# A dense layer as seven block products instead of eight: Strassen's scheme in the second layer of an FFT-plus-hardswish kernel

## The chip, the core and the metric

The kernel runs on one core of a Trainium2 chip. Its engines are TensorE (PE in the profile; PEld is its weight load), VectorE (DVE), ScalarE (ACT), GpSimd (POOL) and SyncE (SP), each with its own instruction queue, worked off in order; 16 DMA engines move data. The metric is the device time of one execution in microseconds (us), as the median of several runs. Everything is f32; TensorE runs each f32 matmul as two passes, so the profile counts two MATMUL and two LDWEIGHTS instructions for each matmul of the code.

## The reference

```python
# x: (8, 3008, 256) f32; w_in: (256, 2048); w_out: (2048, 256), both f64
X = np.fft.fft(np.fft.fft(x, axis=1), axis=2).real.astype(np.float32)
h = X.reshape(8 * 3008, 256) @ w_in
g = h * np.clip(h + 3.0, 0.0, 6.0) / 6.0
out = (g @ w_out).astype(np.float32)          # (24064, 256)
```

Two discrete Fourier transforms, of length 3008 over the sequence and 256 over the features, of which the real part is kept, then two dense layers with a hardswish between them. The second dense layer, g @ w_out, is what the change recasts.

## The kernel before, in words

**Transforms.** The sequence transform is split as 3008 = 47 x 64. The eight batches are worked off in four pairs (class Pair). Stage 1 (load_x, fold, stage1) takes the 47-point transform as a matmul with a constant matrix F: load_x (L97) brings a piece of 8 of the 64 columns n2 on GpSimd's DMA queue, fold (L102) adds and subtracts mirrored features on VectorE for the first pair and on GpSimd for the others, stage1 (L114) multiplies, ScalarE copies out of PSUM, and SP stores the piece to a tensor zd in DRAM. Stage 2 (load_g, stage2, stage2n_mul, stage2n_sum, L131 to L167) reads zd back in groups by output frequency k1 (load_g, on GpSimd's queue), takes the 64-point transform with the data as stationary operand, and leaves q and a correction row qn in SBUF; the small product m of stage2n_mul runs on VectorE. The feature transform never runs by itself: fold_w_in multiplies it into the first layer's weights at the start (W1, and WN for the one feature that is handled apart).

**The dense layers.** A pair's tokens come in 6 chunks (class Chunk) of 8 rows k1 x batch with 64 tokens each, and each chunk stands for twice its 512 tokens: by symmetry u + v is the layer's input sum for one frequency and u - v that of the mirrored one. For each block fc of 128 of the 2048 hidden features a step does this:

- mlp1 (L177): u and v, one matmul of 512 columns each, into one PSUM bank each (ps_h, one buffer of each); VectorE forms s = u + WN * qn (L189), h[0] = s + v (L191) and h[1] = s - v, tokens reversed (L193), all to SBUF; ScalarE forms t = relu(h / 6 + 0.5) for both (L195).
- gate (L198): a = min(t, 1) * h on VectorE, twice (L202), t and h both in SBUF.
- mlp2 (L206): eight matmuls, each with 128 tokens of a as stationary operand and the 256 columns of W2 of this fc as moving operand (L213), summed over the 16 fc in four PSUM banks. After the last fc ScalarE copies each bank out (L222) and SP stores it in rows of 1 KB (L230, L233). The last chunk of a pair has six k1 rows in its mirrored half, so seven matmuls.

**The order** is written out by hand. Step number s runs over 4 pairs x 6 chunks x 16 fc = 384. In each step the program emits, in this order: what beside() has put there for this step, mlp1 of step s + 2, gate of step s + 1, mlp2 of step s. Each engine's queue follows that order. beside() spreads the other work over the steps: for the first pair the reading (load_w_out) and narrowing (narrow_w_out) of the w_out blocks 2 to 7 at steps 0 to 11; in every pair the load of the next g groups and their stage 2; and for the pair that comes next, its load_x, its folds on GpSimd and its stage 1.

**The start.** Before step 0 the kernel loads constants and the first pair's x, runs its stage 1, and loads and narrows w_in. The weights arrive as f64; narrow (L259) turns one block of 512 columns into f32 with eight VectorE operations (L271 to L278) on SBUF. Blocks 0 and 1 of w_out are narrowed before step 0, straight into W2.

Of the kernel before, what the change touches and what calls it, by code (L numbers as in the profile page):

```python
# [26 lines left out]

N1, N2 = 47, 64
NK1 = (N1 + 1) // 2


@with_exitstack
def kernel(
# [14 lines left out]
    NFC = FF // P  # L48
    NP = B // 2
    PR, PZ = 2 * N1, 4 * NK1  # L50
    XC = 8
    NXC = N2 // XC
    KC = 8
# [3 lines left out]
    assert NXC == 2 * FF // 512 and NFC % 2 == 0  # L57
    assert S == N1 * N2 and D == 2 * P and B % 2 == 0 and TB == 512 and NK1 % KK == 0
# [5 lines left out]
    wpool = ctx.enter_context(tc.tile_pool(name="wpool", bufs=1))  # L64
# [3 lines left out]
    hpool = ctx.enter_context(tc.tile_pool(name="hpool", bufs=2))  # L68
    apool = ctx.enter_context(tc.tile_pool(name="apool", bufs=3))
    opool = ctx.enter_context(tc.tile_pool(name="opool", bufs=4))  # L70
# [6 lines left out]
    out_k = out.rearrange("(b k2 k1) d -> b k2 k1 d", b=B, k1=N1)  # L77
# [3 lines left out]
    F = consts.tile([PR, PZ], F32, name="F")  # L81
# [4 lines left out]
    W2 = consts.tile([P, NFC, D], F32, name="W2")  # L86
# [26 lines left out]

    def stage1(pr, c, i):  # L114
# [6 lines left out]
        ps = ps_d.tile([P, 2, D], F32, tag="d", name="ps1")  # L121
        nc.tensor.matmul(ps[0:PZ], F[:], y[:, 2 * i:2 * i + 2, :], start=True, stop=True)  # L122
# [8 lines left out]
    def load_g(pr, ck):  # L131
        g = gpool.tile([P, 2, KK, D], F32, tag="g", name="g")
        for b in range(2):
            nc.gpsimd.dma_start(  # L134
                out=g[:, b],
                in_=pr.zd[b].rearrange("k c n d -> (c n) k d")[:, ck * KK:(ck + 1) * KK, :],
            )
        pr.g[ck] = g

    def stage2(pr, ck, i):  # L140

        if i == 0:
            pr.q[ck] = qpool.tile([P, 2, KC, N2], F32, tag="q", name="q")
        g = pr.g[ck]
        ps = ps_d.tile([P, 2, 4, N2], F32, tag="d", name="ps2")
        for u in range(4):
            kk, b = 2 * i + u // 2, u % 2
            for blk in range(2):
                nc.tensor.matmul(ps[:, blk, u], g[:, b, kk, blk * P:(blk + 1) * P],  # L149
                                 T[:, blk, ck * KK + kk], start=True, stop=True)  # L150
        nc.scalar.copy(pr.q[ck][:, :, 4 * i:4 * i + 4, :], ps[:])  # L151

    def stage2n_mul(pr, ck):

        m = spool.tile([P, KK, 2, N2], F32, tag="m", name="m")
        t0 = T[:, 0, ck * KK:(ck + 1) * KK, :].unsqueeze(2).to_broadcast([P, KK, 2, N2])
        gn = pr.g[ck][:, :, :, P:P + 1].rearrange("p b k o -> p k b o").to_broadcast([P, KK, 2, N2])
        nc.vector.tensor_tensor(m[:], t0, gn, op=AL.mult)
        pr.pr[ck] = m

    def stage2n_sum(pr, ck):
        m = pr.pr.pop(ck)
        ps = ps_d.tile([P, TB], F32, tag="d", name="ps3")
        nc.tensor.matmul(ps[:], ones[:], m[:].rearrange("p k b n -> p (k b n)"), start=True, stop=True)  # L164
        pr.qn[ck] = qpool.tile([P, TB], F32, tag="qn", name="qn")
        nc.scalar.copy(pr.qn[ck][:], ps[:])  # L166
        del pr.g[ck]  # L167

    class Chunk:
        def __init__(self, pr, ck):  # L170
            self.pr, self.ck = pr, ck
            self.nm = KC - 2 if ck == NCK - 1 else KC

            self.tiles = [(0, j) for j in range(KC // 2)] + [(1, j) for j in range(self.nm // 2)]
            self.h, self.t, self.a, self.acc = {}, {}, {}, {}

    def mlp1(ch, fc):  # L177
        q, qn = ch.pr.q[ch.ck], ch.pr.qn[ch.ck]
        fs = slice(fc * P, (fc + 1) * P)
        u = ps_h.tile([P, TB], F32, tag="u", name="u")  # L180
        v = ps_h.tile([P, TB], F32, tag="v", name="v")
        nc.tensor.matmul(u[:], W1[:, 0, fs], q[:, 0], start=True, stop=True)  # L182
        nc.tensor.matmul(v[:], W1[:, 1, fs], q[:, 1], start=True, stop=True)  # L183
        s = spool.tile([P, KC, N2], F32, tag="s", name="s")
        h = hpool.tile([P, 2, KC, N2], F32, tag="h", name="h")
        t = hpool.tile([P, 2, KC, N2], F32, tag="t", name="t")
        nm = ch.nm
        v3 = v[:].rearrange("p (k n) -> p k n", n=N2)
        nc.vector.scalar_tensor_tensor(s[:].rearrange("p k n -> p (k n)"), qn[:], WN[:, fc:fc + 1], u[:],  # L189
                                       op0=AL.mult, op1=AL.add)  # L190
        nc.vector.tensor_tensor(h[:, 0], s[:], v3, op=AL.add)  # L191

        nc.vector.tensor_tensor(h[:, 1, 0:nm, ::-1], s[:, 0:nm], v3[:, 0:nm], op=AL.subtract)  # L193
        for sg, n in ((0, KC), (1, nm)):
            nc.scalar.activation(t[:, sg, 0:n], h[:, sg, 0:n], AF.Relu, bias=half[:], scale=1.0 / 6.0)  # L195
        ch.h[fc], ch.t[fc] = h, t

    def gate(ch, fc):  # L198
        h, t = ch.h.pop(fc), ch.t.pop(fc)
        a = apool.tile([P, 2, KC, N2], F32, tag="a", name="a")  # L200
        for sg, n in ((0, KC), (1, ch.nm)):
            nc.vector.scalar_tensor_tensor(a[:, sg, 0:n], t[:, sg, 0:n], 1.0, h[:, sg, 0:n],  # L202
                                           op0=AL.min, op1=AL.mult)
        ch.a[fc] = a

    def mlp2(ch, fc):  # L206
        a = ch.a.pop(fc)
        last = fc == NFC - 1
        for i, (sg, j) in enumerate(ch.tiles):

            if fc == 0 and i % 2 == 0:
                ch.acc[i // 2] = ps_a.tile([P, 2, D], F32, tag="acc", name="acc")
            nc.tensor.matmul(ch.acc[i // 2][:, i % 2],  # L213
                             a[:, sg, 2 * j:2 * j + 2, :].rearrange("p k n -> p (k n)"), W2[:, fc, :],
                             start=(fc == 0 and i % 2 == 0), stop=last, skip_group_check=True)
            if last and (i % 2 == 1 or i == len(ch.tiles) - 1):
                store(ch, i // 2)

    def store(ch, m):
        ts = ch.tiles[2 * m:2 * m + 2]  # L220
        o = opool.tile([P, 2, D], F32, tag="o", name="o")
        nc.scalar.copy(o[:, 0:len(ts)], ch.acc[m][:, 0:len(ts)])  # L222
        ks = [(ch.ck * KK + j + 1) % NK1 for _, j in ts]
        ks = [N1 - k if sg else k for (sg, _), k in zip(ts, ks)]
        for b in range(2):
            rows = out_k[2 * ch.pr.p + b]
            src = o[b * N2:(b + 1) * N2]
            if len(ks) == 2 and abs(ks[1] - ks[0]) == 1:
# [236 lines left out]
```

## Time and profile before

| | |
|---|---|
| median of 3 runs | 2261.85 us (2255.24 to 2263.06) |
| profiled execution | 2265.05 us, its span 2263.3 us |
| granted TensorE clock, mean | 0.991 |
| busy: PE, PEld | 2217.8 us, 1591.3 us |
| busy: DVE, ACT, POOL | 1389.2 us, 675.2 us, 181.4 us |
| HBM read, written | 60.07 MB, 49.81 MB |

How to read it: the chain of waits is followed back from the last instruction, at each step to what released it or to the instruction before it on its engine, so its shares tell what the time is made of. A group row gives line, engine, operation, output <- inputs, shapes and count, then the busy time and the mean length of one, then the idle time of the engine just before these instructions and what ended most of it. A timeline row gives start and length in us, the engine, line and operation, and how many instructions are merged into it. Matmuls overlap in TensorE's pipe, so the distance from one start to the next tells what they cost. An idle engine that is not on the chain costs nothing.

### The profile page before, as it was taken

The numbers are of one execution on the slowest core, as the hardware profiler recorded it, in microseconds if no ns is written. First come the engines' busy times: TensorE is split into PE (matmuls) and PEld (weight loads), VectorE is DVE, ScalarE is ACT, GpSimd is POOL, SyncE is SP. The second block draws the span as 40 slices with busy tenths as digits, with TensorE's granted clock in tenths as the row PEclk, the third lists the DMA queues.
The fourth block names the chain that finished last, engine by engine and source line by source line (L and its number), as shares of the span: only waits on it lengthen the run. The fifth ranks groups of instructions, "written<-read, shape, count | busy, mean of one in ns | idle before, by whom it ended". The sixth has DMA issues, their size and how long they took to land.

```text
span 2263.3 us, 22686 instructions
## 1 busy us (share of the span) xinstructions
PE 2217.8 (98%) x8720; PEld 1591.3 (70%) x8720; DVE 1389.2 (61%) x2097; ACT 675.2 (30%) x1077; POOL 181.4 (8%) x157
## 2 busy tenths in 40 slices
PE   6799999999999999999999999999999999999998
PEld 2467777777777777777777777777777777777776
DVE  6686656656665666655755665665566565665664
ACT  2223333232222332323222323233232232232322
POOL 0201112102000111110200111120000000000000
PEclk9799999999999999999999999999999999999999
DMA  8611112112110221111310111121101000100000
GB/s 251 194 55 47 47 50 72 51 33 79 38 30 1 61 71 54 46 33 47 84 33 17 46 47 47 47 79 33 52 19 29 26 19 25 32 19 1 19 19 17
DMA packets 39659, 111.35 MB, mean 49 GB/s; under 512 B 5440, under 2 KB 18496, under 8 KB 33344
## 3 DMA queue, kind: packets, MB, share of 16 engines
q1 hardware_dynamic: 28912, 58.51, 9.6%
q0 software_dynamic: 10496, 49.81, 7.7%
q8 instruction: 70, 1.15, 0.2%
q10 hardware_dynamic: 144, 1.57, 0.2%
q14 instruction: 37, 0.30, 0.0%
HBM read 60.07 MB, written 49.81 MB: 49 GB/s over the span
## 4 chain that ended last, share of the span: by engine, by line
PE 97%; DVE 2%; DMA 1%; issue 0%; ACT 0%; SPq 0%; POOL 0%; ACTq 0%; DVEq 0%
PE acc L213 57%; PE u L182 15%; PE v L183 15%; PE ps L122 5%; PE ps L149 4%; PE ps L164 1%; DMA st<-in_moe_w_in_dram 1%; PE wps L314 1%; DMA g<-zd 0%; DMA st<-in_moe_w_out_dram 0%; PE wns L320 0%; DVE low L272 0%; DVE ex L277 0%; DVE ex L276 0%; DVE top L271 0%; DVE frac L273 0%
## 5 line engine op out<-in xcount | busy, mean ns | idle before, releaser
L213 PEld LDWEIGHTS acc<-W,a 128*128 128x128 f32 x6016 | 1143.9, 190 | 319.7 <-issue 181.2
L213 PE MATMUL acc<-W,a 128*128 128x256 f32 x6016 | 1362.1, 379 | 0.0
L195 ACT ACTIVATE t<-h,half 128x512 f32<-128x512 f32 (+1 forms) x768 | 505.6, 705 | 1138.4 <-DVE h L191 1138.4
L189 DVE SCALAR_TENSOR_TENSOR s<-qn,WN,u 128x512 f32<-128x512 f32 x384 | 286.9, 747 | 778.4 <-PE u L182 778.4
L202 DVE SCALAR_TENSOR_TENSOR a<-t,h 128x512 f32<-128x512 f32 (+1 forms) x768 | 543.2, 749 | 0.0
L182 PE MATMUL u<-q,W 128*128 128x512 f32 x768 | 397.2, 598 | 10.4 <-DVE s L189 10.4
L183 PE MATMUL v<-q,W 128*128 128x512 f32 x768 | 394.0, 595 | 0.4 <-DVE h L193 0.4
L191 DVE TENSOR_TENSOR h<-s,v 128x512 f32<-128x512 f32 x384 | 264.2, 688 | 43.4 <-PE v L183 1.3
L183 PEld LDWEIGHTS v<-q,W 128*128 128x128 f32 x768 | 145.8, 190 | 186.4 <-issue 105.0
L193 DVE TENSOR_TENSOR h<-s,v 128x512 f32<-128x512 f32 (+1 forms) x384 | 252.7, 658 | 0.0
L182 PEld LDWEIGHTS u<-q,W 128*128 128x128 f32 x768 | 142.8, 191 | 84.6 <-issue 60.7
L122 PE MATMUL ps<-y,F 94*96 94x512 f32 x256 | 136.3, 632 | 19.7 <-DMA F<-in_c_stage_dram 15.6
L123 ACT COPY z<-ps 96x512 f32<-96x512 f32 x128 | 74.5, 582 | 225.5 <-PE ps L122 225.5
L108 POOL TENSOR_TENSOR y<-xt 94x1016 f32<-94x1016 f32 x24 | 56.3, 2345 | 973.7 <-PE ps L122 927.0
L149 PEld LDWEIGHTS ps<-T,g 128*128 128x128 f32 x768 | 96.4, 198 | 10.1 <-issue 7.3
L149 PE MATMUL ps<-T,g 128*128 128x64 f32 x768 | 94.5, 278 | 7.5 <-issue 7.2
L134 POOL DMA_DIRECT2D g<-zd x48 | 36.8, 771 | 757.5 <-PE ps L149 452.0
L122 PEld LDWEIGHTS ps<-y,F 94*96 94x96 f32 x256 | 42.4, 172 | 49.5 <-issue 25.2
L151 ACT COPY q<-ps 128x512 f32<-128x512 f32 x48 | 28.1, 586 | 149.6 <-PE ps L149 149.6
L110 POOL TENSOR_TENSOR y<-xt 94x1016 f32<-94x1016 f32 x24 | 57.4, 2393 | 0.1
L222 ACT COPY o<-acc 128x512 f32<-128x512 f32 x96 | 48.4, 575 | 5.5 <-PE acc L213 5.5
L166 ACT COPY qn<-ps 128x512 f32<-128x512 f32 x24 | 14.1, 586 | 45.2 <-PE ps L164 45.2
(30 smaller groups left out, 229.2 us busy)
## 6 DMA issues: line engine op xcount, KB each, us to landing
zd<-z SPq DMA_DIRECT2D x32, 768.0 KB, 4.3
g<-zd POOLq DMA_DIRECT2D x48, 512.0 KB, 5.1
xt<-in_x_dram POOLq DMA_DIRECT2D x32, 752.0 KB, 5.6
out_dram<-o SPq DMA_DIRECT2D x176, 128.0 KB, 2.4
st<-in_moe_w_in_dram SPq DMA_DIRECT2D x8, 512.0 KB, 8.3
st<-in_moe_w_out_dram SPq DMA_DIRECT2D x8, 512.0 KB, 5.1
T<-in_c_stage_dram ACTq DMA_DIRECT2D x1, 1536.0 KB, 9.0
out_dram<-o SPq DMA_DIRECT2D x24, 64.0 KB, 2.0
```

Source lines behind the costliest of these rows:

```text
L110: eng.tensor_tensor(y[:, :, P + 1:D], lo, hi, op=AL.subtract)
L122: nc.tensor.matmul(ps[0:PZ], F[:], y[:, 2 * i:2 * i + 2, :], start=True, stop=True)
L123: nc.scalar.copy(z[:, 2 * i:2 * i + 2, :], ps[0:PZ])
L149: nc.tensor.matmul(ps[:, blk, u], g[:, b, kk, blk * P:(blk + 1) * P], T[:, blk, ck * KK + kk], start=True, stop=True)
L182: nc.tensor.matmul(u[:], W1[:, 0, fs], q[:, 0], start=True, stop=True)
L183: nc.tensor.matmul(v[:], W1[:, 1, fs], q[:, 1], start=True, stop=True)
L189: nc.vector.scalar_tensor_tensor(s[:].rearrange("p k n -> p (k n)"), qn[:], WN[:, fc:fc + 1], u[:], op0=AL.mult, op1=AL.add)
L191: nc.vector.tensor_tensor(h[:, 0], s[:], v3, op=AL.add)
L193: nc.vector.tensor_tensor(h[:, 1, 0:nm, ::-1], s[:, 0:nm], v3[:, 0:nm], op=AL.subtract)
L195: nc.scalar.activation(t[:, sg, 0:n], h[:, sg, 0:n], AF.Relu, bias=half[:], scale=1.0 / 6.0)
L202: nc.vector.scalar_tensor_tensor(a[:, sg, 0:n], t[:, sg, 0:n], 1.0, h[:, sg, 0:n], op0=AL.min, op1=AL.mult)
L213: nc.tensor.matmul(ch.acc[i // 2][:, i % 2], a[:, sg, 2 * j:2 * j + 2, :].rearrange("p k n -> p (k n)"), W2[:, fc, :], start=(fc == 0 and ...
```

## The change

The second layer's product G @ W is split into 2 x 2 blocks and formed by the Winograd form of Strassen's scheme: seven block products in place of eight, with four sums on the side of g, four on the side of the weights and seven on the products.

- **Blocks.** A step now has two blocks of hidden features, fc and fc + 8, and a chunk 4 rows instead of 8 (KC = 4, 256 columns, 12 chunks a pair, 8 steps each: again 384 steps). The two halves of tokens are the plain and the mirrored one; the two halves of output features are interleaved in blocks of 32.
- **mlp1** runs four matmuls of 256 columns (two blocks for u, two for v). u and v are tiles of one tag with three PSUM buffers. s is formed by two VectorE operations of 256; the sum and the difference are written back over u and v in PSUM; the relus read them there; and the two gates follow at once, inside mlp1, with t in SBUF and u or v in PSUM. The mirrored half carries a minus sign, which the sums take up.
- **combine** is new: GpSimd forms the four sums of the g blocks in three operations of 512, 256 and 256 elements. It takes the place of gate in the emission order (for step s + 1, after mlp1 of step s + 2).
- **mlp2** runs seven matmuls with weights stationary (the tile G, seven combinations of w_out blocks) and 256 columns of a or c moving, 192 in a pair's last chunk. The products lie in the four banks of ps_a; after a chunk ScalarE copies them to a tile e.
- **finish** and **store** are new in this form: in the next chunk's steps 0, 1 and 2, GpSimd forms the output blocks with seven sums in five operations (finish), VectorE transposes 32 x 32 blocks (two operations for each token half), and SP stores in pieces of 256 bytes, 16 DMAs a chunk.
- **mix_w_out** is new: four VectorE and four ScalarE operations for each pair of w_out blocks form G. Narrowing now takes one block in each of steps 0 to 5, with a mix in steps 1, 3 and 5; mix 0 stands before step 0.
- **Moved or cut otherwise:** x pieces and stage 1 in units of 4 columns with three x buffers (XC = 4); load_g on SP's queue; stage2n_mul on GpSimd; one PSUM bank (ps_d) for stages 1 and 2, but the four of ps_a until step 0.

The diff, cut to its core:

```diff
-    XC = 8
+    XC = 4
-    KC = 8
+    KC = 4
...
-    xpool = ctx.enter_context(tc.tile_pool(name="xpool", bufs=2))
+    xpool = ctx.enter_context(tc.tile_pool(name="xpool", bufs=3))
...
-    ps_d = ctx.enter_context(tc.tile_pool(name="ps_d", bufs=2, space=PSUM))
-    ps_h = ctx.enter_context(tc.tile_pool(name="ps_h", bufs=1, space=PSUM))
+    ps_d = ctx.enter_context(tc.tile_pool(name="ps_d", bufs=1, space=PSUM))
+    ps_h = ctx.enter_context(tc.tile_pool(name="ps_h", bufs=3, space=PSUM))
...
-            nc.gpsimd.dma_start(
+            nc.sync.dma_start(
                 out=g[:, b],
...
-        nc.vector.tensor_tensor(m[:], t0, gn, op=AL.mult)
+        nc.gpsimd.tensor_tensor(m[:], t0, gn, op=AL.mult)
...
     def mlp1(ch, fc):
+        u = ps_h.tile([P, 2, KC, N2], F32, tag="uv", name="u")
+        v = ps_h.tile([P, 2, KC, N2], F32, tag="uv", name="v")
+        for blk, ps in ((0, u), (1, v)):
+            for i in range(2):
+                f = fc + i * NF
+                nc.tensor.matmul(ps[:, i], W1[:, blk, f * P:(f + 1) * P], q[:, blk, of:of + KC],
+                                 start=True, stop=True)
...
+        nc.vector.tensor_tensor(u[:, :, 0:ns], s[:, :, 0:ns], v[:, :, 0:ns], op=AL.add)
+        relu(t[:, 0, :, 0:ns], u[:, :, 0:ns], 1.0 / 6.0)
...
+        nc.vector.tensor_tensor(v[:, :, 0:nm], v[:, :, 0:nm], s[:, :, 0:nm], op=AL.subtract)
+        relu(t[:, 1, :, 0:nm], v[:, :, 0:nm], -1.0 / 6.0)
+        gate(a[:, 0, :, 0:ns], t[:, 0, :, 0:ns], u[:, :, 0:ns])
...
+            gate(a[:, 1, i, 0:nm, ::-1], t[:, 1, i, 0:nm], v[:, i, 0:nm])
...
+    def combine(ch, fc):
+        a = ch.a[fc][:].rearrange("p m f k n -> p (m f) (k n)")[:, :, 0:ch.n]
+        c = cpool.tile([P, 4, TB], F32, tag="c", name="c")
+        cn = c[:, :, 0:ch.n]
+        add(cn[:, 0:2], a[:, 2:3].to_broadcast([P, 2, ch.n]), a[:, 3::-3])
+        add(cn[:, 2], cn[:, 0], a[:, 0])
+        add(cn[:, 3], a[:, 1], cn[:, 2])
+        ch.c[fc] = cn
+
+    def add(out, in0, in1):
+        nc.gpsimd.tensor_tensor(out, in0, in1, op=AL.add)
...
     def mlp2(ch, fc):
+        moving = [a[:, 0], a[:, 1], a[:, 3], c[:, 0], c[:, 1], c[:, 2], c[:, 3]]
+        for i, mv in enumerate(moving):
...
+            nc.tensor.matmul(ch.acc[i // 2][:, i % 2, 0:ch.n], G[:, i, fc, :], mv,
+                             start=(fc == 0 and i % 2 == 0), stop=(fc == NF - 1), skip_group_check=True)
...
+                nc.scalar.copy(ch.e[:, k:i + 1, 0:ch.n], ch.acc[i // 2][:, 0:i + 1 - k, 0:ch.n])
+
+    def finish(ch):
...
+        add(rn[:, 0, 0], e[:, 0], e[:, 1])
+        add(wn[:, 0], e[:, 0], e[:, 5])
+        add(wn[:, 1:3], wn[:, 0:1].to_broadcast([P, 2, n]), e[:, 4:2:-1])
+        add(rn[:, 0, 1], wn[:, 2], e[:, 6])
+        add(rn[:, 1], wn[:, 1:2].to_broadcast([P, 2, n]), e[:, 2:4])
...
     def store(ch, m):
+        for h in range(2):
+            nc.vector.transpose(o[:, 0:n // DH, h], ch.r[:, m, h, 0:n].rearrange("p (j i) -> p j i", i=DH))
...
+            for qd in range(DB):
+                nc.sync.dma_start(
...
+    def mix_w_out(j):
...
+        tt(w[3], b11, b12, op=AL.subtract)
+        tt(t2[:], b22, w[3], op=AL.add)
+        tt(w[2], t2[:], b21, op=AL.subtract)
+        tt(w[4], b22, b12, op=AL.subtract)
...
             for j in range(2, NWO):
-                put(0, 2 * j - 4, narrow_w_out, j)
+                put(j - 2, narrow_w_out, ORDER[j])
...
+                if j % 2:
+                    put(j - 2, mix_w_out, j // 2)
...
         if s + AHEAD < len(steps):
             mlp1(*chunk(s + AHEAD))
         if s + 1 < len(steps):
-            gate(*chunk(s + 1))
+            combine(*chunk(s + 1))
+        if prev and fc < 3:
+            finish(prev) if fc == 0 else store(prev, fc - 1)
         mlp2(*chunk(s))
```

More of the change, by code (lines that the diff above doesn't have):

```diff
@@ L219, in store @@
-    def store(ch, m):
[L220 to L228, printed above, removed]
-                st = ks[1] - ks[0]
-                nc.sync.dma_start(out=rows[:, ks[0]:ks[0] + 2 * st:st, :], in_=src)
-            else:
-                for r, k in enumerate(ks):
-                    nc.sync.dma_start(out=rows[:, k:k + 1, :], in_=src[:, r:r + 1])
+                ch.acc[i // 2] = ps_a.tile([P, 2, TB], F32, tag="acc", name="acc")
@@ L397 @@
     mlp1(*chunk(1))
-    gate(*chunk(0))
+    combine(*chunk(0))
+    prev = None
     for s, (p, ck, fc) in enumerate(steps):
@@ L401 @@
             at = beside(p)
[L402 removed]
+        for f, a in at.get(ck * NF + fc, ()):
             f(*a)
```

263 lines of the change are left out of this document (157 added, 106 removed).

## The prediction, made before the changed kernel ran

> **What bounds the kernel now.** I read the page's head and chain first, then the groups by line, then the timeline of one steady stretch engine by engine, then the start and the end.
>
> ```profile
> span 2263.3 us, 22686 instructions
> ...
> PE 2217.8 (98%) x8720; PEld 1591.3 (70%) x8720; DVE 1389.2 (61%) x2097; ACT 675.2 (30%) x1077; POOL 181.4 (8%) x157
> ...
> PE 97%; DVE 2%; DMA 1%; issue 0%; ACT 0%; SPq 0%; POOL 0%; ACTq 0%; DVEq 0%
> PE acc L213 57%; PE u L182 15%; PE v L183 15%; PE ps L122 5%; PE ps L149 4%; PE ps L164 1%; DMA st<-in_moe_w_in_dram 1%; PE wps L314 1%; DMA g<-zd 0%; DMA st<-in_moe_w_out_dram 0%; PE wns L320 0%; DVE low L272 0%; DVE ex L277 0%; DVE ex L276 0%; DVE top L271 0%; DVE frac L273 0%
> ...
> L213 PEld LDWEIGHTS acc<-W,a 128*128 128x128 f32 x6016 | 1143.9, 190 | 319.7 <-issue 181.2
> L213 PE MATMUL acc<-W,a 128*128 128x256 f32 x6016 | 1362.1, 379 | 0.0
> L195 ACT ACTIVATE t<-h,half 128x512 f32<-128x512 f32 (+1 forms) x768 | 505.6, 705 | 1138.4 <-DVE h L191 1138.4
> ```
>
> TensorE carries 97% of the chain, 57% in the second dense layer (L213). Every f32 matmul is two passes, so L213's 6016 are 3008 matmuls. What a pass costs is read from the starts in the timeline of a steady stretch, not from the 379 ns, which overlap:
>
> ```profile
> 248.59 1.90 PE L149 MATMUL ps<-T,g 128*128 128x64 f32 x16
> 250.32 1.08 PE L182 MATMUL u<-q,W 128*128 128x512 f32 x2
> ...
> 256.41 1.02 PE L182 MATMUL u<-q,W 128*128 128x512 f32 x2
> ...
> 258.12 3.62 PE L213 MATMUL acc<-W,a 128*128 128x256 f32 x16
> ...
> 261.58 1.02 PE L182 MATMUL u<-q,W 128*128 128x512 f32 x2
> ...
> 267.61 1.02 PE L182 MATMUL u<-q,W 128*128 128x512 f32 x2
> ```
>
> A plain step is 261.58 - 256.41 = 5.17 us: 1.71 for u and v, 3.46 for 16 passes, 0.216 per pass of 256 columns. The next step, 6.03 (261.58 to 267.61), has one stage-1 matmul more (0.86). Half a stage 2 takes 1.73 (248.59 to 250.32). TensorE has no gap here; a step costs the sum of its passes.
>
> **Passes on TensorE.** The change keeps 384 steps. First layer: 8 passes of 256 columns for 4 of 512, the same columns, 1.72. Its weight loads double, but L213 already hides a 190 ns load under each 216 ns pass, so this costs nothing; if it did not hide, L213 would be slower today. Second layer: 7 products by 2 passes, 14 for 16, 3.02. A step becomes 4.74. The last of a pair's chunks now moves 192 columns: 14 x 0.216 x 0.75 = 2.26, a step 3.98 (bound: 3.02 if a narrow pass costs a full one, +24 us in all; the 64-column passes at 1.73 / 16 = 0.108 say it does not). Today's last chunk of a pair has 14 passes, by the chain of waits near the end:
>
> ```profile
> 2241.95 3.02 PE acc L213 x14
> ```
>
> Before: 320 x 5.17 + 64 x 4.74 = 1958. After: 352 x 4.74 + 32 x 3.98 = 1796. **-162 us.** Stages 1 and 2 keep their passes.
>
> **VectorE's step.** The timeline of one step, VectorE's add and the relu on ScalarE that it releases:
>
> ```profile
> 2000.48 0.69 DVE L191 TENSOR_TENSOR h<-s,v 128x512 f32<-128x512 f32 x1
> ...
> 2001.26 1.33 ACT L195 ACTIVATE t<-h,half 128x512 f32<-128x512 f32 x2 [3.84 <-DVE h L191]
> ```
>
> The gates now stand in mlp1, behind their own relu. From these rows: s in two halves about 0.95 (0.86 today, L189 to L191 below, plus 0.1 for one more instruction); relu starts 0.78 after the add, takes 0.7, about 0.1 to signal, so gate 0 starts 1.6 after the add and gate 1 ends at 2.9. Together 3.85, plus four transposes of 256 a chunk (no row; half of a 0.69 op each, 0.18 a step). Queued behind the waiting gates is only the next step's s, which waits for TensorE anyway. 4.0 under 4.74: hidden. The add and subtract now write PSUM, which no row shows: between nothing more (L191 reads PSUM at the usual 0.6) and twice as long (+1.2 a step: 5.2, over the 5.0 of steps without stage 1, +44 us). I take the first.
>
> **GpSimd's step**, the new load and the dearest unknown. The timeline of GpSimd in one fold (two sums, two DMA issues between them, a small copy, the next load's issue):
>
> ```profile
> 243.66 2.34 POOL L108 TENSOR_TENSOR y<-xt 94x1016 f32<-94x1016 f32 x1 [40.84 <-PE ps L122]
> 245.95 1.56 POOL L134 DMA_DIRECT2D g<-zd  x2
> 247.53 2.36 POOL L110 TENSOR_TENSOR y<-xt 94x1016 f32<-94x1016 f32 x1
> 249.81 0.70 POOL L111 COPY y<-xt 94x16 f32<-94x16 f32 x1
> 250.46 0.57 POOL L99 DMA_DIRECT2D xt<-in_x_dram  x1
> ```
>
> 1016 elements take 2.29 start to start. Pure proportion gives 1.15 for 512 and 0.58 for 256. If the copy of 16 (0.65) is all fixed cost, 512 cost 1.46 and 256 cost 1.05. That copy jumps 128 elements at each one and the adds run straight, so I stay nearer the first: 1.28 and 0.76. A combine (512 + 256 + 256, two waits on itself at 0.1) is 3.0 (2.5 to 3.8); a finish (2 x 512, 3 x 256) 5.2 (4.1 to 6.5) a chunk. In a chunk that also folds: 8 x 3.0 + 5.2 + two folds of about 3.2 and their load issues (0.57 each) + half a mul (0.65) = 37.4. TensorE's chunk there: 8 x (4.74 + 0.43 stage 1 + 0.27 stage 2 with its sum) = 43.5. Hidden on average. Locally: at the start of every second chunk the queue holds load, combine, finish, then mul (moved here, in front of the next combine): 0.2 + 0.57 + 3.0 + 5.2 + 1.3 + 3.0 = 13.3 us after the step began (0.2 is when the first combine's gates are done). The products that need this second combine come two steps later, behind u, v and three products of a alone: 2 x 5.44 + 1.72 + 1.29 = 13.9. Without load and stage 1 it is 12.7 against 2 x 5.0 + 3.0 = 13.0. A margin of about nothing; I add **+5** (0.2 us at 24 such starts).
>
> The Trainium skill (GPSIMD Engine Reference, section 3.1) gives 4497 ns for an add of 2048 and advises VectorE for such work. With 2.29 at 1016 that makes an estimate of 2.7 to 2.8 a combine; by it the sum would stay without the +5.
>
> **Do the two engines hold each other up?** VectorE's timeline beside that same fold, and one pair of gates (253.50) with no fold beside it:
>
> ```profile
> 244.48 0.75 DVE L189 SCALAR_TENSOR_TENSOR s<-qn,WN,u 128x512 f32<-128x512 f32 x1 [2.69 <-PE u L182]
> 245.34 0.69 DVE L191 TENSOR_TENSOR h<-s,v 128x512 f32<-128x512 f32 x1
> ...
> 246.54 4.52 DVE L202 SCALAR_TENSOR_TENSOR a<-t,h 128x512 f32<-128x512 f32 x2
> ...
> 253.50 1.29 DVE L202 SCALAR_TENSOR_TENSOR a<-t,h 128x512 f32<-128x512 f32 x2
> ```
>
> While GpSimd folds, the ops with one operand in PSUM run at their usual 0.75 and 0.69, but two gates with both inputs in SBUF take 4.52 for 1.29. The new gates read u or v from PSUM and t from SBUF, L189's form, so by these rows they pass freely. The Trainium skill (SBUF — State Buffer, "SBUF: two separate sides") says that GpSimd and a VectorE op with two SBUF inputs lock each other out for a whole instruction; this trace agrees (+3.23 us for two gates). It speaks against the start, where w_out is still narrowed and mixed beside the combines.
>
> **The start.** The chain of waits, then the timeline:
>
> ```profile
> 75.98 5.49 DMA st<-in_moe_w_out_dram
> ```
> ```profile
> 89.35 0.42 DVE L271 TENSOR_SCALAR top<-st 128x512 int32<-128x512 int32 x1
> ...
> 93.46 0.42 DVE L271 TENSOR_SCALAR top<-st 128x512 int32<-128x512 int32 x1
> ...
> 96.53 1.43 PE L182 MATMUL u<-q,W 128*128 128x512 f32 x2
> ...
> 101.60 0.74 DVE L189 SCALAR_TENSOR_TENSOR s<-qn,WN,u 128x512 f32<-128x512 f32 x1
> ...
> 107.94 2.43 POOL L108 TENSOR_TENSOR y<-xt 94x1016 f32<-94x1016 f32 x1 [6.40 <-DMA xt<-in_x_dram]
> 108.09 2.56 DVE L271 TENSOR_SCALAR top<-st 128x512 int32<-128x512 int32 x1
> ...
> 117.91 0.74 DVE L189 SCALAR_TENSOR_TENSOR s<-qn,WN,u 128x512 f32<-128x512 f32 x1
> ...
> 122.28 4.79 PE L213 MATMUL acc<-W,a 128*128 128x256 f32 x16
> ```
>
> A narrow alone is 4.1 (89.35 to 93.46); beside folds 9.8 (108.09 to 117.91), its own time plus GpSimd's two folds: they add. Today six narrows lie in steps 0 to 10 and TensorE runs unbroken from 122.28, having done four u,v pairs and one second-layer step, 10.3 us: 112 us lost. After: load_g moves to SP's queue and the mul to GpSimd, so the first two narrows no longer wait for g and start when their rows land (81.5), end near 90, mix 0 (four ops, no row; 0.42 each from half a 0.69 op and a signal: 1.7) near 92, and s(0) waits only for u: 98 instead of 101.6. Two steps of VectorE: 105.6. Then a narrow stands in each of steps 0 to 5, ahead of mlp1, and a mix in every second. Each combine becomes ready just as VectorE starts narrowing, so they take turns: 6 x (4.1 + 3.85 + 3.0) + 3 x 1.7 + 5.6 (two load issues, mul, fold, by turns too) = 76 us, to 182. By then TensorE has done 8 x 1.72 + 0.86 + 6 x 3.02 + 1.7 + 1.7 = 36 us: 146 lost. **+34 us** (with no turn-taking 24 less). Stage 1 of pair 0 has the same passes and bytes in smaller pieces, with more PSUM banks; +-4.
>
> **The end and the queues.** SP's last output issues (timeline), the end of the last pass (chain), and the page's DMA parts:
>
> ```profile
> 2254.24 1.13 SPq L230 DMA_DIRECT2D out_dram<-o  x2
> ```
> ```profile
> 2255.33 0.02 issue
> ```
> ```profile
> out_dram<-o SPq DMA_DIRECT2D x176, 128.0 KB, 2.4
> ...
> q1 hardware_dynamic: 28912, 58.51, 9.6%
> ```
>
> From the last pass (2255.3) to the end are 8 us. After: copy 0.3, the first half of a 192-column finish 2.9, two transposes 0.6, 16 issues at 0.57 = 9.1, landing 2.4, signals about 1: 16 to 17. **+9 us.** Inside, 16 issues a chunk (9 us of 40) and the moved load_g leave SP's queue free. The output goes in 96,256 pieces of 256 bytes; q1's packet takes 0.096 x 2263 x 16 / 28912 = 0.12 us of an engine, at most a third of the 16 engines: hidden.
>
> **Sum**, against the profiled execution's 2265.05: -162 + 34 + 9 + 5 = 2151. The median of the runs is 3.2 lower: **2148 us.**
>
> **The rivals.**
> *GpSimd becomes the bound* (all dear ends: combine 3.8, finish 6.5, fold 3.55, mul 1.46): its folding chunk takes 45.5 against 43.5, and 24 such chunks (8 in each of three pairs) cost 48 us; in the other 24 the second combine ends at 15.6 behind a mul and 14.2 without, against 13.0, on average 1.9 late, 46 us. In place of the 5: 2148 + 89 = 2237. For: the margins above. Against: the straight adds.
> *VectorE becomes the bound* (PSUM writes twice as long): 2148 + 44 = 2192. Against: PSUM reads cost nothing extra.
> *The port is shared after all* (slower): the gates wait for GpSimd as L202 did. +3.23 a step makes VectorE 7.3; 376 steps from 182 and 17 at the end, about 2930. It decides from 1.4 us a step (a step of 5.49 would equal today's time). For: L202's row. Against: L189 and L191 beside the same fold.
> *The change saves no TensorE time*: the passes can be counted in the diff, 14 for 16; only a pass that costs more than 0.216 could undo it, and L213 has the same shape. No chance of its own.
>
> **How the numbers follow.** Forecast (TensorE stays the bound, 2119 to 2180) 0.66; GpSimd 0.18; VectorE 0.06; shared port, or a wait among the three u,v banks of that size, 0.10. The range goes from the start without turn-taking and without local stalls (2148 - 24 - 5 = 2119) to 2220, which takes in the VectorE case and the cheaper three quarters of GpSimd's; with a little of the forecast lost at either end about 0.8 lies in it. All but the last are faster by over 0.5%, which is about what a measurement of this kernel can tell from no change; a mild form of the last, or GpSimd dearer than priced, could land within it: faster 0.88, same 0.03, slower 0.09.
>
> **What would show it.** Right: second-layer passes 5376 (4928 of 256 columns, 448 of 192) at 0.216 start to start, plain steps of 4.74 in the last pair, PE over 95% of the chain after about 182 us, gates near 0.7 beside a busy GpSimd, combines near 3.0. Wrong: idle before the products released by POOL (c) or before v released by DVE, gates of over 1 us in the middle of the run, a first unbroken stretch that starts far from 182, or a tail far from 17.

## The result, and the profile after

| | before | after |
|---|---|---|
| median | 2262.45 us (4 runs, 2255.24 to 2267.87) | 2138.09 us (4 runs, 2136.32 to 2139.95) |
| profiled execution, its span | 2265.05 us, 2263.3 us | 2137.45 us, 2135.5 us |
| busy: PE, DVE, POOL | 2217.8, 1389.2, 181.4 us | 2067.8, 1489.9, 1424.5 us |

The changed kernel takes 0.9452 of the time before [0.9424, 0.948]: 124 us less, where 114 were forecast. The page's head and chain, and the passes of the second layer by shape:

```profile
PE 2067.8 (97%) x9616; PEld 1752.6 (82%) x9616; DVE 1489.9 (70%) x2785; ACT 707.4 (33%) x1221; POOL 1424.5 (67%) x1629
...
PE 90%; DVE 5%; DMA 2%; issue 1%; ACT 1%; SPq 0%; POOL 0%; DVEq 0%; POOLq 0%; ACTq 0%
```
```profile
L272 PE MATMUL acc<-c,G 128*128 128x256 f32 x2816 | 666.1, 379 | 0.0
L272 PE MATMUL acc<-a,G 128*128 128x256 f32 x2112 | 518.0, 382 | 0.0
L272 PE MATMUL acc<-c,G 128*128 128x192 f32 x256 | 46.8, 326 | 0.0
L272 PE MATMUL acc<-a,G 128*128 128x192 f32 x192 | 36.4, 326 | 0.0
```

TensorE is still the engine that sets the end. Its second-layer passes are 4928 of 256 columns (2816 + 2112) and 448 of 192. None of these four groups waited: the idle time in the last column is 0.0. GpSimd went from 8% to 67% busy, and stands at 0% in the chain.

One plain step in the timeline:

```profile
2003.71 1.03 PE L218 MATMUL u<-q,W 128*128 128x256 f32 x4
2004.02 1.27 POOL L262 TENSOR_TENSOR c<-a 128x512 f32<-128x512 f32 x1 [1.87 <-PE acc L272]
...
2004.78 0.87 DVE L223 SCALAR_TENSOR_TENSOR s<-qn,WN,u 128x256 f32<-128x256 f32 x2 [0.90 <-PE u L218]
...
2005.44 1.46 PE L272 MATMUL acc<-a,G 128*128 128x256 f32 x6
2005.75 0.70 DVE L231 TENSOR_TENSOR u<-s,v 128x512 f32<-128x512 f32 x1
2006.17 0.73 POOL L262 TENSOR_TENSOR c<-a,c 128x256 f32<-128x256 f32 x1
2006.73 1.89 PE L272 MATMUL acc<-c,G 128*128 128x256 f32 x8
...
2007.94 0.68 DVE L250 SCALAR_TENSOR_TENSOR a<-t,v 128x512 f32<-128x512 f32 x1
2008.46 1.90 PE L173 MATMUL ps<-T,g 128*128 128x64 f32 x16
```

From u at 2003.71 to the next work at 2008.46 are 4.75 us: 1.73 for u and v, 1.29 for six passes, 1.73 for eight. VectorE works from 2004.78 to 2008.62, 3.84 us, and its second gate takes 0.68. GpSimd's combine takes 2.88 (2004.02 to 2006.90). Both lie inside TensorE's step.

The stretches table, for the whole run between start and tail and for two chunks in which GpSimd also folds (a stretch begins where u of a chunk's first step begins):

```profile
core 0: us, PE busy (x) PEld busy (x) DVE busy (x) ACT busy (x) POOL busy (x), PEclk, DMA share, GB/s
170.00:2122.00 1952.00, 1949.49 (x9242) 1679.78 (x9242) 1352.77 (x2536) 662.44 (x1136) 1379.70 (x1573) 1.00 0.17 44
716.96:760.18 43.22, 43.22 (x202) 36.51 (x201) 28.99 (x52) 14.89 (x25) 33.38 (x39) 1.00 0.19 49
760.18:804.26 44.08, 44.08 (x204) 36.89 (x203) 29.00 (x52) 15.49 (x26) 32.38 (x38) 1.00 0.26 72
```

TensorE is busy for 1949.49 of 1952.00 us (and has 97% of the chain there), and for the whole of each folding chunk, in which GpSimd works 32 to 33 us.

The start and the end, in the chain of waits:

```profile
75.84 7.09 DMA g<-zd
...
92.31 0.89 DVE s L223 x2
...
99.77 0.34 DVE top L349
...
106.62 0.80 DVE s L223 x2
...
133.45 0.34 DVE top L349
...
139.57 0.34 DVE G L390
...
166.62 2.04 PE v L218 x4
```
```profile
2115.57 6.51 PE acc L272 x40
```

The first narrowing among the steps begins at 99.77 and VectorE lets TensorE run unbroken from 166.62: 67 us for six steps with their narrowing, combines and three mixes. The last pass ends at 2122.08 (2115.57 + 6.51), 13.4 us ahead of the end.

### The profile page after: what moved, and what is told of

Its sections match the earlier page's. It is cut to its first block, busy times and chain, and to the rows that moved or that the text cites. A ratio compares the mean times of both kernels' runs of the same rounds, so it can differ in the third digit from the quotient of the medians.

```text
span 2135.5 us, 29238 instructions
## 1 busy us (share of the span) xinstructions
PE 2067.8 (97%) x9616; PEld 1752.6 (82%) x9616; DVE 1489.9 (70%) x2785; ACT 707.4 (33%) x1221; POOL 1424.5 (67%) x1629
## 3 DMA queue, kind: packets, MB, share of 16 engines
q1 hardware_dynamic: 144768, 83.72, 14.4%
## 4 chain that ended last, share of the span: by engine, by line
PE 90%; DVE 5%; DMA 2%; issue 1%; ACT 1%; SPq 0%; POOL 0%; DVEq 0%; POOLq 0%; ACTq 0%
PE acc L272 51%; PE v L218 15%; PE u L218 15%; PE ps L145 4%; PE ps L173 4%; PE ps L189 1%; DVE a L250 1%; DMA st<-in_moe_w_in_dram 1%; ACT t L247 1%; DVE u L231 1%; DVE s L223 0%; DVE frac L351 0%; DVE low L350 0%; DVE ex L353 0%; DMA xt<-in_x_dram 0%
## 5 line engine op out<-in xcount | busy, mean ns | idle before, releaser
L262 POOL TENSOR_TENSOR c<-a 128x512 f32<-128x512 f32 (+1 forms) x384 | 478.6, 1246 | 559.2 <-PE acc L272 295.8
L272 PE MATMUL acc<-c,G 128*128 128x256 f32 (+1 forms) x3072 | 713.0, 375 | 0.0
L223 DVE SCALAR_TENSOR_TENSOR s<-qn,WN,u 128x256 f32<-128x256 f32 x768 | 334.3, 476 | 440.2 <-PE u L218 435.5
L272 PEld LDWEIGHTS acc<-c,G 128*128 128x128 f32 x3072 | 578.5, 190 | 73.2
L272 PE MATMUL acc<-a,G 128*128 128x256 f32 (+1 forms) x2304 | 554.4, 377 | 0.0
L272 PEld LDWEIGHTS acc<-a,G 128*128 128x128 f32 x2304 | 437.9, 192 | 57.8
L218 PE MATMUL v<-q,W 128*128 128x256 f32 x1536 | 401.0, 384 | 27.9 <-DVE a L250 27.9
L218 PE MATMUL u<-q,W 128*128 128x256 f32 x1536 | 397.6, 381 | 0.0
L262 POOL TENSOR_TENSOR c<-a,c 128x256 f32<-128x256 f32 (+1 forms) x384 | 276.5, 720 | 30.1
L262 POOL TENSOR_TENSOR c<-c,a 128x256 f32<-128x256 f32 (+1 forms) x384 | 275.4, 717 | 30.1
L231 DVE TENSOR_TENSOR u<-s,v 128x512 f32<-128x512 f32 (+1 forms) x384 | 263.0, 685 | 42.5 <-DVE s L223 2.3
```

What stands on the lines that cost most here:

```text
L218: nc.tensor.matmul(ps[:, i], W1[:, blk, f * P:(f + 1) * P], q[:, blk, of:of + KC], start=True, stop=True)
L223: nc.vector.scalar_tensor_tensor(s[:, i].rearrange("p k n -> p (k n)"), qn[:, of * N2:(of + KC) * N2], WN[:, f:f + 1], u[:, i].rearrange(" ...
L231: nc.vector.tensor_tensor(u[:, :, 0:ns], s[:, :, 0:ns], v[:, :, 0:ns], op=AL.add)
L262: nc.gpsimd.tensor_tensor(out, in0, in1, op=AL.add)
L272: nc.tensor.matmul(ch.acc[i // 2][:, i % 2, 0:ch.n], G[:, i, fc, :], mv, start=(fc == 0 and i % 2 == 0), stop=(fc == NF - 1), skip_group_c ...
```

## Experiments

The theory: TensorE's passes set the time; seven products are worth their share of them because everything added lies under TensorE's step, and what is given back lies in the start and the tail. The rivals: the shared port (gates with both inputs in SBUF) or GpSimd's load would undo the gain. The ratios below are against the kernel before, run on the same chip, with a 95% interval.

**The scheme alone undone.** Everything else of the rewrite stays (chunks of 256 columns, outputs turned over, stores of 256 bytes):

```diff
-        for i, mv in enumerate(moving):        # seven products
+        for q in range(2):
+            for f in range(2):                 # eight plain ones, for both m
+                nc.tensor.matmul(ch.acc[m][:, q, 0:ch.n], G[:, 2 * f + q, fc, :], a[:, 2 * m + f],
...
-            combine(*chunk(s + 1))
...
-    finish(prev)
```

> The changed kernel with only the scheme undone: eight plain block products a step, no combine, no finish, the rest (256-column steps, gates from PSUM, transposes, start) as changed. If the gain is the passes that TensorE no longer runs (theory): 352 steps x 0.431 + 32 x 0.324 = 162 us more, less about 16 at the start (narrowing no longer takes turns with combines), 7 (no mix on VectorE) and 4 at the end (no finish): 2138 + 162 - 27 = 2273, between 2260 and 2290; second-layer passes 6144 and a plain step of 5.17 us. If the gain came from the rest of the rewrite (rival): it stays near 2138, at most 2180.

Measured: 2264.98 us, 1.0005 [0.9996, 1.0015].

The rest of the rewrite comes to nothing in sum; the seven products are worth all of it, 127 us. By passes alone they would be worth more: this kernel has 5632 of 256 columns and 512 of 192, against 4928 and 448, and 704 x 0.216 + 64 x 0.163 = 162 us, 40.5 for each pair. What they give back is seen in the starts of u of the two profiled executions. The second pair begins 17.3 us later here (650.1 for 632.8) and not 40.5, so 23 us are given back by then, nearly all in the start, where combines and mixes stand beside the narrowing (the granted clock was lower there too, 0.81 for 0.91 between 80 and 180 us). Each of the next two pairs takes 39.2 us more, so 1.4 a pair are lost in a wait that the next experiment shows. The last pair and the tail give back 3.8, since the tail is 10.0 for 13.4 us (finish). Together that is 30 of the 162. The profiled executions differ by 132 and not by 127, because this kernel's was the longest of its ten runs.

**The rival that ends slower: gates with both inputs in SBUF.** The sum goes to a tile of its own and the difference over s:

```diff
+        u = spool.tile([P, 2, KC, N2], F32, tag="h", name="h")
...
-        nc.vector.tensor_tensor(v[:, :, 0:nm], v[:, :, 0:nm], s[:, :, 0:nm], op=AL.subtract)
+        nc.vector.tensor_tensor(s[:, :, 0:nm], v[:, :, 0:nm], s[:, :, 0:nm], op=AL.subtract)
+        v = s
```

> The sum and the difference go to SBUF instead of back into PSUM, so both gates have two SBUF inputs again, as in the kernel before; all else as changed. Port shared at the price of the prediction's slower rival (each pair of gates +3.23 us): VectorE's step 7 us, about 2900 us. Port shared, but a gate waits only for the rest of one GpSimd operation, and not when GpSimd is idle: gates of 0.9 to 1.5 us on average instead of 0.69, VectorE's step 4.2 to 5.2, 2145 to 2250. No sharing: gates 0.69, 2138.

Measured: 2130.89 us, 0.9414 [0.94, 0.9428]: 7 us faster than the changed kernel, where none of the three cases had it faster. The gates by groups (of 512 elements), of the changed kernel and then of this one:

```profile
L250 DVE SCALAR_TENSOR_TENSOR a<-t,u 128x512 f32<-128x512 f32 x352 | 241.8, 687 | 96.6 <-ACT t L247 91.9 <-POOL c L262 4.7
L250 DVE SCALAR_TENSOR_TENSOR a<-t,v 128x512 f32<-128x512 f32 x352 | 239.4, 680 | 0.0
```
```profile
L252 DVE SCALAR_TENSOR_TENSOR a<-t,h 128x512 f32<-128x512 f32 x352 | 311.3, 884 | 64.0 <-ACT t L249 50.7 <-POOL c L264 1.8 <-POOL r L264 0.5
L252 DVE SCALAR_TENSOR_TENSOR a<-t,s 128x512 f32<-128x512 f32 x352 | 352.1, 1000 | 0.0
```

The gates are held, as the rival says: 0.88 and 1.00 us on average against 0.69 and 0.68. But that is half a microsecond a step, not 3.23. This kernel's timeline shows why, first beside a fold and the small copy behind it, then in a plain step:

```profile
848.76 1.27 POOL L125 TENSOR_TENSOR y<-xt 94x508 f32<-94x508 f32 x1
849.47 1.12 DVE L252 SCALAR_TENSOR_TENSOR a<-t,h 128x512 f32<-128x512 f32 x1 [0.20 <-ACT t L249]
849.97 0.67 POOL L126 COPY y<-xt 94x8 f32<-94x8 f32 x1
...
1998.68 0.69 DVE L252 SCALAR_TENSOR_TENSOR a<-t,s 128x512 f32<-128x512 f32 x1
...
1999.52 1.27 POOL L264 TENSOR_TENSOR c<-a 128x512 f32<-128x512 f32 x1 [1.87 <-DVE a L252]
```

In a plain step a combine waits for its gates and is over when the next ones come, so the two keep out of each other's way by themselves. A gate is held where other work of GpSimd fills the time between, or where that work has made a combine late. In the last pair, which has no folds, nearly all held gates lie in four of a chunk's eight steps, beside the finish of the chunk before and the combines behind it. From 200 us on, 358 of the 677 gates of 512 elements last under 0.75 us. VectorE's step is then some 4.4 us on average (3.84 and the 0.52 more for two gates), still under 4.75, and TensorE's steps stay at 4.75. The lock works the other way too: the copy of 8 elements takes 0.67 us where it stands beside such a gate, and 0.20 in the changed kernel. The Trainium skill (SBUF — State Buffer, "SBUF: two separate sides") has GpSimd and such a VectorE operation lock each other out; the held gates agree, and here the lock stayed within the slack and cost no time.

Where the gain comes from is seen in a pair's last chunk, of the changed kernel and then of this one:

```profile
2110.34 1.10 PE L218 MATMUL v<-q,W 128*128 128x256 f32 x4 [0.45 <-DVE a L250]
...
2114.46 1.10 PE L218 MATMUL v<-q,W 128*128 128x256 f32 x4
```
```profile
2100.15 1.03 PE L218 MATMUL v<-q,W 128*128 128x256 f32 x4
...
2104.15 1.03 PE L218 MATMUL v<-q,W 128*128 128x256 f32 x4
```

With the gates reading PSUM, v waits for a bank until the last gate has read it (the 0.45 in brackets), and the step takes 4.12 us (2110.34 to 2114.46), in steps with transposes up to 4.69. With SBUF copies the bank is free after the difference, and the step takes 4.00. By the starts of u, the last chunks' steps give 5.6 of the 6.4 us between the two profiled executions.

**Is it GpSimd that makes the scheme pay?** The combine's three sums on VectorE instead:

```diff
-        add(cn[:, 0:2], a[:, 2:3].to_broadcast([P, 2, ch.n]), a[:, 3::-3])
+        tt = nc.vector.tensor_tensor
+        tt(cn[:, 0:2], a[:, 2:3].to_broadcast([P, 2, ch.n]), a[:, 3::-3], op=AL.add)
...
```

> The three sums of combine on VectorE instead of GpSimd. If VectorE has no room for them (theory): its step becomes 3.7 + 0.6 + 2 x 0.35 + waits 0.2 + transposes 0.2 = 5.4 us against 5.0 for TensorE in the 24 chunks without folds and 5.44 in those with: +77 us, less some 7 at the start, about 2205; more, up to 2300, if the sums (two SBUF inputs) also wait for folds and finish. If it does not matter which engine forms the sums (rival): 2138, plain steps 4.74.

Measured: 2347.52 us, 1.0376 [1.0361, 1.0392], slower than the kernel before. Head and chain of its page, and one step of its timeline:

```profile
PE 2135.1 (91%) x9616; PEld 1731.0 (74%) x9616; DVE 2136.8 (91%) x3937; ACT 697.9 (30%) x1221; POOL 444.9 (19%) x477
...
DVE 61%; PE 16%; ACT 9%; issue 5%; SPq 4%; DMA 3%; DVEq 1%; ACTq 0%; POOL 0%; POOLq 0%
```
```profile
2004.81 1.03 PE L218 MATMUL u<-q,W 128*128 128x256 f32 x4
...
2006.16 1.10 PE L218 MATMUL v<-q,W 128*128 128x256 f32 x4 [0.32 <-DVE a L250]
2006.54 0.68 DVE L257 TENSOR_TENSOR c<-a 128x512 f32<-128x512 f32 x1
...
2007.71 0.42 DVE L259 TENSOR_TENSOR c<-a,c 128x256 f32<-128x256 f32 x1
...
2010.12 1.03 PE L218 MATMUL u<-q,W 128*128 128x256 f32 x4
```

This plain step takes 5.31 us, of which VectorE's sums are 1.52 (0.68 and twice 0.42). VectorE has next to no gap left in it: it is 91% busy over the span and has 61% of the chain, and TensorE waits for it (the 0.32 in brackets, v for the bank that the gates free; 165.7 us over the run). So VectorE sets the step. I had expected about 2205, and up to 2300 if the sums also wait for folds and finish. They do wait: after 200 us the sum of 512 takes 0.68 us on average where GpSimd is idle and 1.20 where it works, and those of 256 take 0.43 and about 0.9. By the starts of u, a chunk without folds (in the last pair) takes 45.0 us for 39.8 or 40.6, and one with folds 46.9 to 48.5 for 43.2 to 44.1, where I had counted no loss. How much of the 209 us is the sums themselves and how much their waits was not tried apart. Undisturbed, the sums are quicker on VectorE (0.68 for 512 against 1.27), and yet the kernel takes 209 us more with them there.

**How much room has GpSimd?** A further sum in each combine, of 256 or of 512 elements, whose output nothing uses:

```diff
+        add(junk[:, 0:2, 0:ch.n], a[:, 0:2], a[:, 2:4])     # 512; with 0:1 and 2:3 it is 256
```

> One more GpSimd sum of 256 elements (0.8 us) behind each combine, its result unused. By the rows of the changed kernel GpSimd's folding chunk becomes 8 x 3.66 + 5.0 + 5.5 + 1.1 + 0.55 = 41.5 us against TensorE's 43.5: no loss on average; at chunk starts the second combine ends at 14.2 against 13.9 and 13.6 against 13.0: 0 to 12 us, 2138 to 2150. If GpSimd were already the bound: 384 x 0.8 = 307 us more, 2445.

> One more GpSimd sum of 512 elements (1.35 us) behind each combine, its result unused. GpSimd's folding chunk becomes 8 x 4.21 + 5.0 + 5.5 + 1.1 + 0.55 = 45.8 us against 43.5: 24 x 2.3 = 55 us; in the other 24 chunks the second combine comes 1.7 late behind a mul and 0.6 without: 28 us. Together 2138 + 83 = 2220 (2190 to 2240), with idle of TensorE released by GpSimd. If GpSimd has more room than its rows say: 2140.

Measured: 2140.05 us, 0.9452 [0.9437, 0.9468], with 256, and 2150.25 us, 0.9495 [0.9477, 0.9513], with 512. The first costs 2 us, within the 0 to 12 expected; the second costs 12 where I expected 82, so GpSimd had more room than I gave it. The same stretches as above, in the kernel with 512 (its steps lie some 9 us later):

```profile
725.70:769.66 43.96, 43.46 (x202) 36.43 (x201) 29.02 (x52) 14.89 (x25) 42.52 (x46) 1.00 0.19 48
769.66:813.74 44.08, 44.08 (x204) 36.89 (x203) 29.02 (x52) 15.49 (x26) 42.65 (x47) 1.00 0.26 72
```

GpSimd is at 42.5 of 44 us, as good as full, and TensorE loses 0.6 to 0.8 us in every second chunk (43.96 for 43.22). By the starts of u in the two profiled executions, the kernel with 512 falls behind the one with 256 by 4.7 us up to the ninth step (1.6 of it before the first step, ahead of any combine), by 1.5 in the rest of the first pair, by 2.8 in each of the next two, and by nothing in the last pair, which has no folds. I had priced GpSimd's folding chunk at 45.8 us, 2.3 over TensorE's 43.5, and 55 us of the loss stood on that. It is 42.5 us of work and 1.1 of load issues in 44. Just where two engines stand level, these 2 us, 5% of the chunk, make 55 us into some 7. Of the 28 us that I had added for the chunks without folds, about half a microsecond a pair is seen.

**Is TensorE still the bound with another product less?** The seventh product is left out, and the sum that it enters takes the sixth in its place:

```diff
-        moving = [a[:, 0], a[:, 1], a[:, 3], c[:, 0], c[:, 1], c[:, 2], c[:, 3]]
+        moving = [a[:, 0], a[:, 1], a[:, 3], c[:, 0], c[:, 1], c[:, 2]]
...
-        add(rn[:, 0, 1], wn[:, 2], e[:, 6])
+        add(rn[:, 0, 1], wn[:, 2], e[:, 5])
```

> The seventh product is left out of every step, and its sum takes the sixth in its place, so the output lacks that part: 12 passes a step. If TensorE is still the bound with room behind it (theory): another 162 us less, 1976, plain steps 4.31 us; VectorE needs 3.9 and GpSimd 35 us of a folding chunk's 40. If another engine or the three u, v banks stand close behind TensorE (rival): steps stay near 4.7 and the time above 2050.

Measured: 1986.88 us, 0.878 [0.8767, 0.8793]. Its timeline:

```profile
1902.46 1.03 PE L218 MATMUL u<-q,W 128*128 128x256 f32 x4
...
1906.78 1.03 PE L218 MATMUL u<-q,W 128*128 128x256 f32 x4
```

A plain step is 4.32 us, two passes of 0.216 less, so neither VectorE nor GpSimd becomes the bound there. Most of the 11 us above the forecast lies in the last chunks, where VectorE held the bank already: there several steps keep their 4.12 to 4.69 us with a product less. A middle pair takes 467.0 or 466.8 us, where 505.47 less 40.6 for its passes would be 464.9; that is some 8 us in four pairs. The rest was not traced.

**The start: narrow and mix everything early.** All of w_out is narrowed and mixed between the pieces of stage 1 of the first pair, with a fourth buffer for its loads:

```diff
+        elif c:
+            k = c // 2 - 1
+            narrow_w_out(ORDER[k])
+            load_w_out(ORDER[k + 1])
+            if k % 2:
+                mix_w_out(k // 2)
...
-                put(j - 2, narrow_w_out, ORDER[j])
...
-                    put(j - 2, mix_w_out, j // 2)
```

> All blocks of w_out are loaded, narrowed and mixed during stage 1 of the first pair, one narrow in every second x piece, none beside the first steps. If the start is lost to VectorE, which narrows by turns with the combines (theory): unbroken passes from about 112 us with 5 us of steps done, instead of 166.6 with 36: 20 to 25 us less, 2113 to 2120. If the start is bound by its transfers (rival): the 3 MB moved ahead push the first step back by as much as is saved, 2133 to 2145.

Measured: 2127.76 us, 0.9399 [0.9383, 0.9414], between the two. The stretches table of its start:

```profile
80.00:100.00 20.00, 15.06 (x35) 5.84 (x34) 19.25 (x42) 6.09 (x14) 0.00 (x0) 0.62 0.55 162
100.00:120.00 20.00, 17.51 (x68) 13.18 (x67) 7.09 (x16) 4.90 (x11) 1.05 (x1) 0.70 0.40 126
```

Unbroken passes now begin at 127 instead of 167, but with much less done by then (the first u comes at 117.6 for 90.8). VectorE is full until 100 us (19 of every 20), so stage 1 itself comes later, and then VectorE idles through the way of the last piece over DRAM and stage 2 (7.09 of 20). So the narrowing was moved from one place where VectorE is full to another, and it seems that only the turns with GpSimd are saved. The granted clock was lower there too, 0.57 to 0.65 between 40 and 100 us, where the changed kernel had 0.95 or more until 80; what that costs was not tried by itself.

**The tail.** With that start, the second half of the last chunk's stores goes to ScalarE's queue:

```diff
-    for m in range(2):
-        store(prev, m)
+    for m, eng in enumerate((nc.sync, nc.scalar)):
+        store(prev, m, eng)
```

> As the early narrowing, and the last chunk's second half of stores on ScalarE's queue, so that the 16 last issues (0.6 us each) run on two queues: by both theories another 3 to 4 us less than the early narrowing alone.

Measured: 2124.91 us, 0.9385 [0.937, 0.9401], 2.9 less than without, about as expected: the 16 issues at 0.46 us each stood one behind the other. From the last u to the end the profiled executions take 19.3 us for 21.5.

**Fill the gap.** Four blocks early, the other four with two mixes in the wait for g, and the split tail:

```diff
+        elif c % 4 == 2:
+            k = c // 4
...
+    for k in range(4, 8):
+        narrow_w_out(ORDER[k])
+        if k % 2:
+            mix_w_out(k // 2)
```

> As the early narrowing with the split tail (2125), but only four blocks of w_out are narrowed during stage 1 and four, with two mixes, in the 20 us between the last fold and the first u, when VectorE waits for stage 2 anyway. If the start is bound by VectorE's work up to the last fold (theory; it was busy 18.8 to 19.3 of every 20 us there): four narrows and two mixes, 20 us, leave that stretch, unbroken passes from 105 to 112 us instead of 127, 2105 to 2112. If transfers bound it (rival): at most 7 us less, 2118 or more.

Measured: 2117.22 us, 0.9344 [0.9331, 0.9358]: a gain (7.7 us by the medians, on another chip; 9 by the ratios), but short of the theory and just under the rival's 2118. The chain of waits:

```profile
93.02 8.24 DMA g<-zd
...
112.46 0.79 DVE s L223 x2
```

The first s now waits for the last mix (until 112.46; stage 2 was done at 109.4), and g takes 8.24 us, with three loads of w_out issued just ahead of it, where it took 4.95 with the loads spread over stage 1. That the loads slow it is likely, but was not tried by itself.

**Both together.** The last kernel with the SBUF sums, and one buffer of c fewer:

```diff
-    cpool = ctx.enter_context(tc.tile_pool(name="cpool", bufs=3))
+    cpool = ctx.enter_context(tc.tile_pool(name="cpool", bufs=2))
```

> As the fill variant, and the sums of u and v in SBUF (both gate inputs in SBUF) with two buffers for c instead of three. The SBUF sums alone took 7 us off the changed kernel, 4 of it by steps of 4.00 instead of 4.12 us in the 32 steps of the last chunks: 5 to 7 us less than the fill variant. If GpSimd and VectorE now hold each other up (rival, since nothing else is left to hide it): no gain or a loss beside the fill variant.

Measured: 2108.05 us, 0.9306 [0.9291, 0.9322], on the same chip as the last: 9 us less, the best of all, 30 us under the changed kernel. The profiled executions differ by 10.8 us. Some 5 of them lie in the steps of the last chunks, as in the first run with SBUF sums. Another 5 were there when TensorE began to run unbroken (114.2 for 119.3), and 2.6 of these, in the last stage 1 of the start, lie ahead of anything that the edit touches, so they are no gain of the edit.

## Why the prediction was right, and where its sizes were off

The mechanism was right: fewer passes at a nearly unchanged price, everything added hidden in all but the narrow steps, something given back at both ends. The forecast for the profiled execution was 2151 us; it took 2137.45. By the prediction's own steps:

- **Passes on TensorE, right but for 9.5 us.** The counts are as forecast, a plain step takes 4.75 for 4.74, and the 192-column passes cost 0.163 each, in proportion. By the starts of u, a pair takes 505.47 us where the old 543.58 less the forecast's 40.5 would be 503.1, **9.5 us too low** over the run. Of the 2.4 us a pair, 1.4 are a wait that the prediction missed in the last chunk, whose step it put at 3.98. VectorE's step there has three operations more (the sum is split, and the gates are four), the split-off one waits for a relu, and the gates hold the bank of v; the SBUF run got these 1.4 back (504.03).

```profile
2108.71 0.30 DVE L234 SCALAR_TENSOR_TENSOR u<-s,v 128x128 f32<-128x128 f32 x1 [0.71 <-ACT t L247]
```

  The other 1.0 is the first layer: its 768 passes of 256 columns a pair take 166.4 us from start to start, where the 384 of 512 took 165.5. So the shorter passes, which the prediction had at nothing, cost 4 us over the run, and the first experiment's kernel has them too (544.62 a pair for 543.58). Whether the doubled weight loads cause it was not tried.
- **VectorE's step, right**: 3.84 for 3.85. The value taken for the PSUM writes (nothing extra) holds: 0.70 and 0.69 us.
- **GpSimd's step**: a combine of 2.88 for 3.0. A finish takes 4.8 for 5.2:

```profile
1034.78 0.73 POOL L262 TENSOR_TENSOR r<-e 128x256 f32<-128x256 f32 x1
...
1039.54 1.27 POOL L262 TENSOR_TENSOR c<-a 128x512 f32<-128x512 f32 x1
```

  The **+5 us** of local stalls is not there: TensorE is busy for all of the folding chunks shown, and its 2.5 us of idle time between 170 and 2122 us lie in the last chunks. The prediction's upper bounds came from the copy of 16 elements, read as fixed cost. In the kernel before, all but one of these copies take over 0.65 us and stand beside VectorE operations with SBUF inputs, mostly the gates; in the second run copies of 8 take 0.65 to 0.67 beside such gates and, but for one, 0.19 to 0.20 otherwise. So the 0.65 was mostly a wait, and the dear prices drawn from it (1.46 and 1.05 for 512 and 256 elements) were too high: 1.27 and 0.73 were measured. (By its own terms the GpSimd rival's folding chunk also comes to 45.9, not 45.5.) With 3.0 and 5.2 the margin was near nothing; with the real durations the queue of 13.3 us is 12.4 (twice 0.12 less for combines, 0.44 for the finish, 0.2 for the mul, which took 1.07), and the two steps of lead suffice. The GpSimd rival falls with it, and the 512 run shows how near it was: 1.27 us more a step, and the engine is full.
- **Shared port.** Right that gates with one input in PSUM pass freely (0.69, 0.68). Wrong in the rival's price: its own form, built in the second run, costs 0.5 us a step, not 3.23, and ends faster, not at 2930. The price was read where VectorE stood beside a queue of folds of 2.3 us each.
- **The start, 15 us too dear**: unbroken from 166.62 for 182. The first s came at 92.31 for 98: g started earlier (75.84), with pieces of half the size that land in 3.0 us for 4.3. The six steps took 67 for 76. GpSimd's work does hold the narrowing, as forecast, but not by its full length: a narrowing of 4.1 alone takes 6.1 us beside a combine (133.45 to 139.57) and 6.9 beside a combine and the mul (99.77 to 106.62), 7.1 with a fold in the mul's place. So a combine of 3 us adds 2, a fold or mul of 1.2 to 1.4 adds 0.9, and the load issues add nothing that can be seen: 40 us for the six narrowings in place of 48.
- **The tail, 3 us too dear**: 13.4 for 16.5. The first of finish's sums runs under the last passes, and an issue took 0.46 us, not 0.57:

```profile
2121.41 0.59 POOL L262 TENSOR_TENSOR r<-e 128x192 f32<-128x192 f32 x1
...
2125.42 7.40 SPq L304 DMA_DIRECT2D out_dram<-o  x16
```

Together: 2151 - 15 - 3 - 5 + 9.5 = 2137.5. The sizes that were off partly cancelled, so it is in part luck that the sum came this near; the start alone was off by more than the whole miss.

## What to carry to other kernels

A scheme that trades matmuls for sums pays when the sums go to an engine with empty time, however slow it is there, and when each lies inside the step of the engine that sets the time: here moving three sums to an engine nearly twice as slow decided between 5% faster and 4% slower. Price a lock between two engines by the instructions that will really stand beside each other, and compare it with the slack: here half the gates were held and no time was lost. And look at the odd places, a pair's narrow last chunk, the start and the tail: the steady step came out to a hundredth, and nearly the whole miss lay in these.

## What the runs showed of the hardware that was not expected

- GpSimd's fixed cost is small: sums take 1.27 us for 512 elements and 0.73 for 256, which leaves some 0.2 (an estimate from these two), and a copy of 8 takes 0.20. Beside gates with two SBUF inputs the same copy takes 0.65 to 0.67, and the copy of 16 in the kernel before 0.65 to 0.71.
- Transposing 32 x 32 blocks costs VectorE as much as a sum of that size in SBUF, 0.42 us for 256 elements (176 transposes, 420 ns on average).
- Stores of 256 bytes instead of 1 KB did no harm: the queue, which took over the loads of g as well, went from 28912 packets to 144768 and from 9.6% to 14.4% of the DMA engines, a store of 32 KB landed in 1.6 us, and the kernel with these stores and eight products took as long as the one before.
